# Softmax sums to 128 rows by one on-chip transfer instead of two through memory, with larger booked margins for small transfers

## The chip, the cores and the metric

The kernel runs on one core of a Trainium2 chip. The metric is the device time of one execution in microseconds (us), median of three runs. The engines of the core are named as in the profile: PE is the matrix engine (PEld its weight loads), DVE the vector engine, ACT the scalar engine, POOL the general engine, and SP the engine that issues nearly all transfers here.

## The reference, cut to what matters

A transformer block of 2048 tokens and width 512, in bfloat16: attention with 32 heads of 16 columns, then a gated feed-forward part of inner width 1792. Both are conditioned by a vector `c`.

```python
mod = silu(c) @ w_mod                         # six rows of 512: sa, ca, ga, sb, cb, gb
h = layernorm(x) * (1 + ca) + sa
q, k, v = heads(h @ wqkv)                     # 32 heads of 16
p = softmax(q @ k.T * 16 ** -0.5)
x = x + ga * (merge(p @ v) @ wo)
h = layernorm(x) * (1 + cb) + sb
x = x + gb * ((gelu(h @ w_gate) * (h @ w_up)) @ w_down)
```

## The kernel before, in words

**The main strand.** The queries are cut into six sets (`SETS`: three of 512 tokens, one of 256, two of 128). For each set and each group of four heads (`qd`, a "unit") the score matmuls put slabs of 128 keys by 512 columns into PSUM (`ps_sc`), ACT takes the exponential of two or three slabs by one instruction (`E<-ps_sc`, 128x1024 or 128x1536), and PE multiplies the result with the values (`ps_pv<-E,vaug`). Each head's value columns carry a column of ones, so that the softmax sum comes out as a 17th row. Some rounds are taken from ACT: there DVE makes one slab of the exponential out of the scores by integer arithmetic (`dreg<-ps_sc`, `mreg<-ps_sc`), and four shifted copies of four such slabs (`mreg<-dreg`, `mreg<-mreg`) are multiplied with scaled values (`ps_pv<-mreg,vs`) to even out the error. Four such slabs are a quad. Where a quad has a slab, ACT's instruction has two slabs instead of three.

**The end of a unit** (`unit_end`, L1576). DVE copies the sums of products to `osb`. Rows 16, 48, 80 and 112 of it are the four softmax sums of up to 512 tokens each. So that DVE can invert them on 128 rows instead of four, they are spread: SP writes them to a scratch tensor in memory (`scr_den<-osb`, stream `da`), waits until they are there, and reads them back on 128 rows of `den` (`den<-scr_den`, stream `db`). DVE inverts (`rden<-den`, L352). SP writes the inverse to memory (`scr_rec<-rden`, `dc`) and reads it back four times, once for each head, repeated over 16 rows (`rb<-scr_rec`, `dd`). DVE multiplies (`onorm<-osb,rb`), and for pairs of units SP moves the second's rows beside the first's (`onorm<-onorm`, `de`). The last two units of each of the two last sets take another way (`near_end`, L950): PE spreads the sums with a selection matrix, and DVE inverts them in place.

**The side strands.** When the units of a set are done, the output projection (`side_wo`, L992), the second layer norm and the feed-forward part (`side_ffn`, L1013; `side_down`, L1120) of that set run on PE and DVE beside the scores of the next set, each part with a position in the main strand by which it is due (`plan`, L1187). Weights are streamed from memory by SP. For the last set but one, the side strand does the first eight of the fourteen inner blocks, and `tail_rest` (L1718) the others. After the last scores, `tail` (L1632) finishes the last two sets.

**What sets the order.** All of it is decided while the program is built. `stream` (L1267) keeps an estimate of when each engine is free and when each result is there (`model`, L248) and puts next what can run next. A transfer is booked as there 900 ns after it can start, plus its size by a rate, plus 1000 ns, or 1500 ns where its runs are 64 bytes or less, plus the `MARGIN` (L49) of its stream. An instruction that needs the transfer is put into its engine's order when the estimate says that the data are there; at run time each engine goes through its list in order, and waits where the data are not. So the bookings decide the order of all five lists, and a changed booking moves instructions on all engines. `step` (L1154) picks DVE's and SP's next tasks, and a quad is begun where ACT, DVE and the side strand's credit allow it.

Of the kernel before, what the change touches and what calls it, by code (L numbers as in the profile page):

```python
# [8 lines left out]
FP32 = mybir.dt.float32  # L9
# [4 lines left out]
P = 128  # L14
# [3 lines left out]
DH = 16  # L18
# [27 lines left out]
FLOW = 3  # L46
URGENT = 9
LATE = 2
MARGIN = {"dd": 700, "de": 700}  # L49
EARLY = 2  # L50
BACK = 8
END = (0, None)
# [28 lines left out]
class _Recorder:  # L81
# [21 lines left out]
    def sb(self, name, shape, dt):  # L103
        t = self.nc.alloc_sbuf_tensor(name, shape, dt)
        n = 1
        for s in shape[1:]:
            n *= s
        self.pitch[name] = n * mybir.dt.size(dt)
        self.kind[name] = "sb"
        return t  # L110
# [262 lines left out]
    def dma(self, eng, out, in_, sem, noncontig=False):  # L373
# [8 lines left out]
        run = min(int(a.ap[-1][1]) * mybir.dt.size(a.dtype) for a in (out, in_))  # L382
        return self.rec(eng, fn, [in_], [out], dma=sem, cost=(n, run, MARGIN.get(sem[:2], 0)))

# [36 lines left out]
class _Kernel(_Recorder):  # L421
# [12 lines left out]
    def alloc(self):  # L434
        sb, ps = self.sb, self.ps
        self.xs = sb("xs", [P, NT, D], BF16)
        self.qT = sb("qT", [P, NDC, S_TOK], BF16)
        self.km = [sb("kme", [P, NDC, S_TOK], BF16), sb("kmo", [P, NDC, S_TOK], BF16)]
        self.vaug = sb("vaug", [P, NKT, H * VW], BF16)
        hreg = sb("hreg", [P, NDC * S_TOK], BF16)  # L440
        self.hT = hreg[:, :].rearrange("p (a n) -> p a n", a=NDC)
        self.prodT = hreg[:, 0:NFC * 512].rearrange("p (f n) -> p f n", f=NFC)
        self.prodL = hreg[:, 0:NFC * 256].rearrange("p (f n) -> p f n", f=NFC)
        self.tb2 = hreg[:, 0:4 * D].rearrange("p (t n) -> p t n", t=4)
        self.tb3 = hreg[:, NFC * 512:NFC * 512 + 2 * D].rearrange("p (t n) -> p t n", t=2)
        wreg = sb("wreg", [P, NDC * 1536], BF16)
        self.wqkv = wreg[:, :].rearrange("p (a n) -> p a n", a=NDC)
        self.t2T = wreg[:, 0:NDC * 512].rearrange("p (a n) -> p a n", a=NDC)
        self.gw = wreg[:, 2048:6144].rearrange("p (b k n) -> p b k n", b=2, k=2)
        mreg = sb("mreg", [P, 2 * NDC * F], BF16)  # L450
        self.wst = [[mreg[:, 1024 * (2 * x + b):1024 * (2 * x + b) + 1024].rearrange("p (a n) -> p a n", a=NDC)
                     for b in range(2)] for x in range(2)]
        self.sq = [mreg[:, 4096 + 2048 * i:6144 + 2048 * i] for i in range(NS)]
        self.wmod = mreg[:, 0:NDC * 3072].rearrange("p (a n) -> p a n", a=NDC)
        dreg = sb("dreg", [P, NFC * D], BF16)
        self.tb1 = dreg[:, 0:8 * D].rearrange("p (b t n) -> p b t n", b=2, t=4)
        self.warm = dreg[:, 8 * D:9 * D]
        self.wdst = [dreg[:, a * D:(a + 2) * D] for a in (8, 10, 12)] + [mreg[:, a * D:(a + 2) * D] for a in (2, 0, 6, 4)]
        self.wdst = [a.rearrange("p (f n) -> p f n", f=2) for a in self.wdst]
        self.wg = [self.qT[:, :, 256 * i:256 * i + 256] for i in range(6)]  # L460
        self.wg.append(hreg[:, NFC * 256:NFC * 256 + 1024].rearrange("p (a n) -> p a n", a=NDC))
        self.wu = [self.wst[i // 2][i % 2] for i in range(4)]
        self.wu += [dreg[:, 1024 * i:1024 * i + 1024].rearrange("p (a n) -> p a n", a=NDC) for i in range(4, 7)]
        self.wd = [self.xs[:, 2 * i:2 * i + 2, :] for i in range(6)]
        self.wd.append(hreg[:, NFC * 256 + 1024:NFC * 256 + 2048].rearrange("p (f n) -> p f n", f=2))
        self.kq = [dreg[:, 0:2048], dreg[:, 2048:4096], mreg[:, 12288:14336]]
        self.vs = sb("vs", [P, len(SHIFT), NKT - T0, H * VW], BF16)
        self.wo = sb("wo", [P, 7, D], BF16)
        self.E = sb("E", [P, NSL, 512], BF16)
        self.onorm = sb("onorm", [P, 8, 512], BF16)  # L470
        self.ga = sb("ga", [P, D], BF16)
        self.gb = sb("gb", [P, D], BF16)
        self.xw = self.gw[:, 0, 0, 0:D]
        self.osb = sb("osb", [P, 1024], FP32)
        self.rb = sb("rb", [P, 1024], FP32)
        self.den = sb("den", [P, 4, 16], FP32)
        self.rden = sb("rden", [P, 4, 16], FP32)
        self.mv = sb("mv", [P, NT, 2], FP32)
        self.st6 = sb("st6", [P, 2, 6], FP32)
        self.rstd = sb("rstd", [P, NT], FP32)  # L480
        self.nwx = sb("nwx", [P, NT], FP32)
        self.nwt = sb("nwt", [P, NT], FP32)
        self.crow = dreg[:, 9 * D:10 * D]
        self.tcol = sb("tcol", [P, NDC], FP32)
        self.sc_bf = sb("sc_bf", [P, NDC], BF16)
        self.scbc = dreg[:, 8 * D:9 * D].rearrange("p (a n) -> p a n", a=NDC)
        self.modA = sb("modA", [P, 8], FP32)
        self.modB = sb("modB", [P, 8], FP32)
        self.rm4 = self.den[:, 0, 0:4]
        self.rm = sb("rm", [P, 2], FP32)  # L490
        self.ident = sb("ident", [P, P], BF16)
        self.ones = dreg[:, 10 * D:10 * D + P]
        self.half = dreg[:, 10 * D + P:10 * D + 2 * P]
        self.self32 = sb("self32", [P, P], FP32)
        self.scp = ps("ps_sc", [P, SC, 512], FP32)
        self.pv = ps("ps_pv", [P, 512], FP32)
        self.mi = ps("ps_mi", [P, 512], FP32)
        self.scr1 = self.dram("scr_den", [4, 2048], FP32)
        self.scr2 = self.dram("scr_rec", [4, 2048], FP32)


# [1074 lines left out]
    def unit_end(self, u, acc):  # L1576
        sets, qd, q0, W = u
        b, lo, hi = self.osb_span(u)
        osb, rb = self.osb[:, lo:hi], self.rb[:, lo:hi]
        assert not self.blocked(u)  # L1580
        self.copy("dve", osb, acc[:, 0:W])
        if sets[0] >= len(SETS) - 2 and len(sets) == 1 and qd >= 6:
            self.done(("osb", sets[0], qd))
            return
        self.live[u] = (lo, hi)
        m = 4 * W // P
        o = 8 if BCOL[sets[0]] else 0
        sem = b + 4 * (o > 0)
        pair = (qd - 1, qd) in self.merged(sets[0])
        s1, s2 = self.scr1[b, P * o:P * o + 4 * W], self.scr2[b, P * o:P * o + 4 * W]  # L1590
        den, rden = self.den[:, b, o:o + m], self.rden[:, b, o:o + m]
        steps = [
            ("sp", lambda: self.dma("sp", s1.rearrange("(j n) -> j n", j=4), self.osb[DH:P:32, lo:hi], "da%d" % sem)),
            ("sp", lambda: self.dma("sp", den, s1.rearrange("(p n) -> p n", p=P), "db%d" % sem)),
            lambda: self.recip(rden, den),
            ("sp", lambda: self.dma("sp", s2.rearrange("(p n) -> p n", p=P), rden, "dc%d" % sem)),
            ]
        steps += [("sp", lambda j=j: self.dma(
            "sp", self.rb[32 * j:32 * j + DH, lo:hi],
            s2[W * j:W * j + W].rearrange("(o n) -> o n", o=1).broadcast_to([DH, W]), "dd%d%d" % (sem, j)))  # L1600
            for j in range(4)]

        def fin2():
            c = OCOL[sets[0]]
            self.tt("dve", self.onorm[:, qd, c:c + W], osb, rb, ALU.mult)
            if self.probing is None:
                self.live.pop(u)
                self.done(("half", u))
                if not pair:
                    for k in sets:  # L1610
                        self.done(("onorm", k, qd))

        def merge(j):
            c = OCOL[sets[0]]
            self.dma("sp", self.onorm[32 * j + DH:32 * j + 2 * DH, qd - 1, c:c + W], self.onorm[32 * j:32 * j + DH, qd, c:c + W],
                     "de%d%d" % (qd // 2, j))
            if self.probing is None and j == 3:
                for k in sets:
                    self.done(("onorm", k, qd))

        def free():
            c = OCOL[sets[0]]
            return ("den", u) in self.have and all(
                ("wo", k) in self.have for k in range(sets[0]) if OCOL[k] < c + W and c < OCOL[k] + SETS[k][1])
        self.task(steps, ("den", u))
        self.task([fin2], ("norm", u), free)
        if pair:
            self.task([("sp", lambda j=j: merge(j)) for j in range(4)], None,
                      self.after([("half", u)] + [("onorm", k, qd - 1) for k in sets]))
# [212 lines left out]
```

## Time and profile before

| | |
|---|---|
| three runs | 864.38, 861.86, 860.3 us; median 861.86 |
| the profiled execution | 861.15 us, of which the span on the core is 859.4 us |
| busy, share of the span | ACT 97%, PE 91%, DVE 82%, POOL 1% |
| transfers | 38.97 MB, 45 GB/s over the span |
| waits of DVE for `den` | 6.4 us in 3 places, the longest 3.8 |
| waits of SP for `scr_den<-osb` | 36.5 us in 32 places |

Times in rows are in us unless marked ns. A row of the timeline begins with its start and its length; in brackets behind it stands how long the engine was idle before it, and what ended that. A row of groups ends with the busy time, the mean of one in ns, and the idle time before.

### The profile page before, as it was taken

The page shows a single profiled execution, that of the slowest core. Times are in us where ns is not written, and L with a number is a line of the kernel's source. Part 1 is how long each engine was busy: PE and PEld are TensorE (multiplying, and loading weights), DVE is VectorE, ACT ScalarE, POOL GpSimd, SP SyncE. Part 2 cuts the span into 40 slices and gives each one's busy share as a digit, 9 for nine tenths or more (in the row PEclk, how much of TensorE's full clock was granted, in tenths as well). Part 3 has the DMA queues.
Part 4 walks back from the last instruction along what each step waited for, and adds up shares of the span by engine and source line. Part 5 has one row for each costly group of instructions (what it writes and reads, how often), then busy time and mean ns, then how long its engine had stood idle before and what let it go on. Part 6 is the DMA issues. An engine that isn't in the chain of part 4 may idle for free.

```text
span 859.4 us, 27732 instructions
## 1 busy us (share of the span) xinstructions
PE 781.9 (91%) x12446; PEld 282.9 (33%) x12446; DVE 703.0 (82%) x1363; ACT 829.8 (97%) x747; POOL 4.5 (1%) x12
## 2 busy tenths in 40 slices
PE   7899999988999989999999899999988898998888
PEld 3333332322222222222222222222333333445456
DVE  7855888888998999999998999999985886677354
ACT  6999999999999999999999999999998999999993
POOL 1000000000000000000000000000000000000000
PEclk9999999999999999999998999999998999999999
DMA  9000000000021111210012112110133122041000
GB/s 309 30 15 17 6 10 11 10 13 9 9 64 38 44 38 42 58 34 24 21 32 64 37 33 60 34 57 20 49 94 107 47 69 80 21 123 43 20 7 15
DMA packets 66169, 38.97 MB, mean 45 GB/s; under 512 B 18657, under 2 KB 63906, under 8 KB 66050
## 3 DMA queue, kind: packets, MB, share of 16 engines
q1 hardware_dynamic: 65520, 36.67, 15.2%
q8 instruction: 97, 1.59, 0.8%
q10 hardware_dynamic: 530, 0.53, 0.2%
q14 instruction: 22, 0.18, 0.1%
HBM read 33.81 MB, written 2.61 MB: 42 GB/s over the span
## 4 chain that ended last, share of the span: by engine, by line
ACT 87%; PE 6%; DVE 3%; DMA 2%; SPq 1%; issue 1%; DVEq 0%
ACT E L328 84%; PE ps_sc L315 3%; ACT wreg L328 3%; PE ps_mi L315 2%; SPq L378 1%; PE ps_pv L315 1%; DMA den<-scr_den 1%; DMA xs<-in_A_x_dram 0%; DMA rb<-scr_rec 0%; DVE xs L332 0%; DVE st L368 0%; DMA mreg<-in_B_w_gate_dram 0%; PE ps_mi L319 0%; DVE dreg L340 0%; DVE nwt L332 0%
## 5 line engine op out<-in xcount | busy, mean ns | idle before, releaser
L328 ACT ACTIVATE E<-ps_sc 128x1536 bf16<-128x1536 f32 (+2 forms) x698 | 803.6, 1385 | 16.3 <-PE ps_sc L315 16.2
L315 PE MATMUL ps_sc<-qT,kmo 32*128 32x512 bf16 (+2 forms) x1408 | 173.8, 325 | 20.3 <-ACT E L328 17.3
L315 PE MATMUL ps_sc<-qT,kme 32*128 32x512 bf16 (+2 forms) x1408 | 170.5, 327 | 19.0 <-ACT E L328 16.9
L315 PE MATMUL ps_pv<-E,vaug 128*17 128x512 bf16 (+2 forms) x2416 | 176.0, 319 | 3.1 <-DVE vaug L349 1.4
L340 DVE TENSOR_SCALAR dreg<-ps_sc 128x512 uint16<-128x512 f32 x200 | 137.6, 690 | 31.7 <-PE ps_sc L315 28.4
L340 DVE TENSOR_SCALAR mreg<-dreg 128x2048 uint16<-128x2048 uint16 x200 | 131.8, 681 | 1.0 <-PE ps_pv L315 0.9
L315 PE MATMUL ps_mi<-wreg,mreg 128*32 128x512 bf16 (+2 forms) x1504 | 112.9, 375 | 12.6 <-DVE wreg L345 6.7
L315 PE MATMUL ps_pv<-mreg,vs 128*17 128x512 bf16 (+1 forms) x1344 | 104.5, 355 | 1.0 <-DVE mreg L340 0.8
L315 PEld LDWEIGHTS ps_sc<-qT,kmo 32*128 32x128 bf16 x1408 | 46.8, 92 | 136.2 <-ACT E L328 109.5
L315 PEld LDWEIGHTS ps_sc<-qT,kme 32*128 32x128 bf16 x1408 | 45.8, 92 | 139.1 <-ACT E L328 112.2
L315 PEld LDWEIGHTS ps_pv<-E,vaug 128*17 128x17 bf16 x2416 | 54.9, 89 | 88.3 <-issue 55.4
L340 DVE TENSOR_SCALAR mreg<-ps_sc 128x512 uint16<-128x512 f32 x96 | 66.2, 690 | 15.6 <-PE ps_sc L315 13.6
L340 DVE TENSOR_SCALAR mreg<-mreg 128x2048 uint16<-128x2048 uint16 x96 | 63.2, 683 | 0.0
L315 PEld LDWEIGHTS ps_mi<-wreg,mreg 128*32 128x32 bf16 (+1 forms) x1504 | 34.7, 96 | 59.6 <-issue 21.8
L349 DVE CAST wreg<-ps_mi 128x512 bf16<-128x512 f32 x51 | 35.0, 687 | 12.4 <-PE ps_mi L315 12.0
L345 DVE SCALAR_TENSOR_TENSOR wreg<-wreg,ps_mi 128x512 bf16<-128x512 bf16 x51 | 34.8, 683 | 12.1 <-ACT wreg L328 7.3
L315 PEld LDWEIGHTS ps_pv<-mreg,vs 128*17 128x17 bf16 x1344 | 32.0, 89 | 29.7 <-DVE mreg L340 14.2
L315 PE MATMUL ps_mi<-hreg,wreg 128*32 128x512 bf16 (+1 forms) x496 | 40.4, 377 | 0.7 <-DVE vaug L349 0.6
L332 DVE TENSOR_TENSOR wreg<-wreg 128x1024 bf16<-128x1024 bf16 (+1 forms) x60 | 35.8, 604 | 0.4
L315 PE MATMUL ps_mi<-mreg,hreg 128*32 128x512 bf16 x384 | 32.5, 384 | 0.0
L315 PE MATMUL ps_sc<-xs,ident 128*32 128x512 bf16 x300 | 25.4, 391 | 7.7 <-ACT E L328 7.3
L328 ACT ACTIVATE wreg<-wreg 128x1024 bf16<-128x1024 bf16 (+1 forms) x30 | 31.9, 1068 | 0.0
(149 smaller groups left out, 571.5 us busy)
## 6 DMA issues: line engine op xcount, KB each, us to landing
mreg<-in_B_w_up_dram SPq DMA_DIRECT2D x25, 256.0 KB, 3.2
mreg<-in_B_w_gate_dram SPq DMA_DIRECT2D x21, 256.0 KB, 2.9
rb<-scr_rec SPq DMA_DIRECT2D x96, 32.0 KB, 1.8
mreg<-in_B_w_down_dram SPq DMA_DIRECT2D x12, 256.0 KB, 2.7
dreg<-in_B_w_down_dram SPq DMA_DIRECT2D x9, 256.0 KB, 4.5
mreg<-in_w_mod_dram SPq DMA_DIRECT2D x1, 2048.0 KB, 12.8
out_dram<-xs SPq DMA_DIRECT2D x15, 128.0 KB, 1.7
xs<-in_A_x_dram SPq DMA_DIRECT2D x3, 512.0 KB, 6.5
```

The source lines that it names most:

```text
L315: return self.rec("pe", lambda e: e.matmul(out, lhsT, rhs, start=start, stop=stop, tile_position=tp), [lhsT, rhs], [out], cost=(n, int(rhs ...
L328: return self.rec("act", lambda e: e.activation(out, in_, func, scale=scale, **kw), rd, wr, cost=self.cost("act", out, [in_], "act"))
L332: return self.rec(eng, lambda e: e.tensor_tensor(out, a, b, op), [a, b], [out], cost=self.cost(eng, out, [a, b], "tt"))
L340: return self.rec(eng, lambda e: e.tensor_scalar(out, a, s1, s2, **kw), rd, [out], cost=self.cost(eng, out, [a], "ts") + (60 if len(rd) > ...
L345: return self.rec("dve", lambda e: e.scalar_tensor_tensor(out, a, s, b, op0=op0, op1=op1), rd, [out], cost=self.cost("dve", out, [a, b], " ...
L349: return self.rec(eng, lambda e: e.tensor_copy(out, in_), [in_], [out], cost=self.cost(eng, out, [in_], "ts"))
L378: return e.dma_start(out, in_)
```

## The change

The four rows of sums are now spread over the 128 rows of `den` by one transfer within the chip's memory: each of the four source rows is read as 32 pieces of `m` numbers (64 bytes for a set of 512 tokens, 32 and 16 for the smaller ones), one piece for each row of `den`. The transfer through `scr_den` and the wait between the two are gone. It is stream `db`, whose margin is now 1000 ns (it had none); the margins of `dd` and `de` grow from 700 to 1000 ns.

```diff
-MARGIN = {"dd": 700, "de": 700}
+MARGIN = {"db": 1000, "dd": 1000, "de": 1000}
...
-        self.scr1 = self.dram("scr_den", [4, 2048], FP32)
...
-        s1, s2 = self.scr1[b, P * o:P * o + 4 * W], self.scr2[b, P * o:P * o + 4 * W]
+        s2 = self.scr2[b, P * o:P * o + 4 * W]
...
-            ("sp", lambda: self.dma("sp", s1.rearrange("(j n) -> j n", j=4), self.osb[DH:P:32, lo:hi], "da%d" % sem)),
-            ("sp", lambda: self.dma("sp", den, s1.rearrange("(p n) -> p n", p=P), "db%d" % sem)),
+            ("sp", lambda: self.dma("sp", den, self.osb[DH:P:32, lo:hi].rearrange("j (a n) -> j a n", n=m), "db%d" % sem)),
```

In the built order this moves instructions on every engine from the first set on. The counts that differ: ACT has 356 exponentials of three slabs and 336 of two, where it had 368 and 324; DVE has 308 slabs of its own, where it had 296, and 308 shifted copies, where it had 296; PE has 128 more `ps_pv<-mreg,vs` and 32 more `ps_pv<-dreg,vaug` of 128 columns, both for the last two sets, and fewer filler products (`xs,ident`: 445 for 496); SP has 40 transfers less.

## The prediction

> **What bounds the kernel now.** I read the page first: the busy times, the chain that ended last, and the granted clock.
>
> ```profile
> PE 781.9 (91%) x12446; PEld 282.9 (33%) x12446; DVE 703.0 (82%) x1363; ACT 829.8 (97%) x747; POOL 4.5 (1%) x12
> PEclk9999999999999999999998999999998999999999
> ACT 87%; PE 6%; DVE 3%; DMA 2%; SPq 1%; issue 1%; DVEq 0%
> L340 DVE TENSOR_SCALAR dreg<-ps_sc 128x512 uint16<-128x512 f32 x200 | 137.6, 690 | 31.7 <-PE ps_sc L315 28.4
> L340 DVE TENSOR_SCALAR mreg<-dreg 128x2048 uint16<-128x2048 uint16 x200 | 131.8, 681 | 1.0 <-PE ps_pv L315 0.9
> L349 DVE CAST wreg<-ps_mi 128x512 bf16<-128x512 f32 x51 | 35.0, 687 | 12.4 <-PE ps_mi L315 12.0
> L345 DVE SCALAR_TENSOR_TENSOR wreg<-wreg,ps_mi 128x512 bf16<-128x512 bf16 x51 | 34.8, 683 | 12.1 <-ACT wreg L328 7.3
> ```
>
> ACT is the bound: 97% busy, and 87% of the chain. So a transfer counts only where its lateness reaches ACT (a wait of DVE holds PE, PE holds the next scores), or after the last exponential. Next, ACT's groups with shapes kept apart, and the timeline of ACT, of which these are rows where it waited in the body:
>
> ```profile
> L328 ACT ACTIVATE E<-ps_sc 128x1536 bf16<-128x1536 f32 x368 | 533.1, 1592 | 6.5 <-PE ps_sc L315 6.4
> L328 ACT ACTIVATE E<-ps_sc 128x1024 bf16<-128x1024 f32 x324 | 333.7, 1165 | 2.6 <-PE ps_sc L315 2.6
> L328 ACT ACTIVATE wreg<-wreg 128x512 bf16<-128x512 bf16 x9 | 6.9, 784 | 0.0
> ...
> 460.96 2.54 ACT L328 ACTIVATE E<-ps_sc 128x1024 bf16<-128x1024 f32 x2 [0.49 <-PE ps_sc L315]
> 463.97 1.02 ACT L328 ACTIVATE E<-ps_sc 128x1024 bf16<-128x1024 f32 x1 [0.48 <-PE ps_sc L315]
> 465.49 21.39 ACT L328 ACTIVATE E<-ps_sc 128x1536 bf16<-128x1536 f32 x19 [0.49 <-PE ps_sc L315]
> 657.44 1.45 ACT L328 ACTIVATE E<-ps_sc 128x1536 bf16<-128x1536 f32 x1 [1.54 <-PE ps_sc L315]
> 659.69 1.02 ACT L328 ACTIVATE E<-ps_sc 128x1024 bf16<-128x1024 f32 x1 [0.80 <-PE ps_sc L315]
> 661.21 2.37 ACT L328 ACTIVATE E<-ps_sc 128x1536 bf16<-128x1536 f32 x2 [0.50 <-PE ps_sc L315]
> 664.45 3.71 ACT L328 ACTIVATE E<-ps_sc 128x1536 bf16<-128x1536 f32 x3 [0.87 <-PE ps_sc L315]
> 778.72 1.45 ACT L328 ACTIVATE E<-ps_sc 128x1536 bf16<-128x1536 f32 x1 [0.94 <-PE ps_sc L315]
> 780.33 5.48 ACT L328 ACTIVATE E<-ps_sc 128x1536 bf16<-128x1536 f32 x4 [0.16 <-PE ps_sc L315]
> 805.91 22.94 ACT L328 ACTIVATE E<-ps_sc 128x1536 bf16<-128x1536 f32 x17 [0.61 <-PE ps_sc L315]
> ```
>
> The brackets are all there is to win from waits: 3.71 from 657 to 664, 1.71 from 778 to 806, 1.46 from 460 to 465. The first and the last of these lie in the two slices where PEclk shows 8 (645 to 666, 451 to 473): there PE itself was slower. What made the two later groups, by the timeline of all engines:
>
> ```profile
> 648.65 3.41 SPq L378 DMA_DIRECT2D onorm<-onorm  x4
> 652.10 0.58 SPq L378 DMA_DIRECT2D den<-scr_den  x1
> 652.72 0.43 SPq L378 DMA_DIRECT2D mreg<-in_B_w_gate_dram  x1
> 655.78 1.07 PE L315 MATMUL ps_mi<-wreg,mreg 128*32 128x512 bf16 x16 [1.79 <-DMA mreg<-in_B_w_gate_dram]
> ...
> 776.14 0.20 DVE L352 RECIPROCAL rden<-den 128x8 f32<-128x8 f32 x1 [1.80 <-DMA den<-scr_den]
> ...
> 803.68 0.18 DVE L352 RECIPROCAL rden<-den 128x4 f32<-128x4 f32 x1 [3.82 <-DMA den<-scr_den]
> ```
>
> At 652.72 a weight load stands on SP behind four `onorm` moves and a `den` read, and PE idles 1.79 for it. At 776.14 and 803.68 DVE waits for `den`.
>
> **Part 1, the transfer.** What a unit pays now, in SP's timeline and the transfers' rows:
>
> ```profile
> 103.95 0.53 SPq L378 DMA_DIRECT2D scr_den<-osb  x1
> 105.66 0.34 SPq L378 DMA_DIRECT2D den<-scr_den  x1
> ...
> q1 hardware_dynamic: 65520, 36.67, 15.2%
> den<-scr_den SPq DMA_DIRECT2D x24, 8.0 KB, 1.6
> DVE rden L352 <- DMA den<-scr_den: 6.4, 3, 3.8
> ```
>
> The first transfer costs 1.71 from its issue to the second's. It goes, 40 times, with 40 issues of 0.53 on SP. The trace shows no transfer from four rows of the chip's memory to 128. Its bounds: 1.6 (what the read of the same 128 pieces takes) and 1.6 plus 0.8. The 0.8 is for a transfer that few of the 16 transfer engines share: q1's 65520 packets took 15.2% of 16 times 859.4, so 31.9 ns each, and 24 more packets in a row take 0.77. I take 2.4. The code books 0.90 + 0.04 + 1.50 + 1.00 = 3.44 for it, where it booked 1.93 and 2.44 for the two; so the planner counts on the sums 0.93 earlier, and the real ones come about 1 before they are counted on. `dd` and `de` get 0.3 more each, so `onorm` is counted on 0.3 to 0.6 earlier. By itself all this is worth nothing to ACT; of the saving only DVE's waits for `den` reach it, 1.71. They go; if that cover is gone, they are back.
>
> There is one rule that speaks against the change. The Trainium skill ("DMA: Bandwidth & Descriptors", "Why a DMA increments its semaphore by 16 and not by 1") says that a transfer is shared by as many engines as divide the outermost sizes of both its sides, so here by 4 and not 16. By it the transfer takes the upper bound above; by 16 engines it would take the lower. No row here shows which. Both lie under the booking, so the sum is the same, but the chance of the slower rival below is larger for it.
>
> **Part 2, the order.** The new lists are in the built kernel. Three differences bear on ACT.
>
> - Three more quads, all in the last three sets: 12 exponentials go from three slabs to two, 12 x (1592 - 1165) = **-5.1**. The price on DVE is 12 x 690 and 12 x 681, 16 in all. DVE has 156 free over the span; in the last stretch this isn't free, see below.
> - In the third weight transition the gate load now stands ahead of the four moves and just behind the `den` transfer, so PE's 1.79 goes, and I count the slow stretch behind it with it, since the clock is down only where PE had stood: -3.7 (1.54, the first bracket alone, if the clock goes down anyway). With the 1.7 from `den` this is **-5.4**.
> - New waits in other places are to be expected, since all lists are new. Nearest rows: one group like that at 460 to 465 (1.46) and one wait like that at 778.72 (0.94): **+2.4**. From nothing to twice the 6.9 lost now.
>
> Until the end of the third set ACT has the same work in both kernels.
>
> **Part 3, the end.** Here the change costs. The rows of the end:
>
> ```profile
> 830.93 8.35 ACT L328 ACTIVATE E<-ps_sc 128x1536 bf16<-128x1536 f32 x6
> 832.38 0.17 DVE L352 RECIPROCAL rden<-den 128x4 f32<-128x4 f32 x1
> 834.82 0.96 DVE L352 RECIPROCAL rb<-ps_mi 128x128 f32<-128x128 f32 x1 [0.58 <-PE ps_mi L315]
> 838.72 0.29 DVE L332 TENSOR_TENSOR onorm<-osb,rb 128x128 bf16<-128x128 f32 x1 [2.62 <-DMA rb<-scr_rec]
> 839.77 0.29 DVE L349 COPY osb<-ps_pv 128x128 f32<-128x128 f32 x1 [0.76 <-PE ps_pv L315]
> 842.76 0.69 DVE L368 BATCH_NORM_STATS2 st<-ps_sc 128x6 f32<-128x512 f32 x1
> 843.70 0.15 DVE L340 TENSOR_SCALAR nwx<-mv 128x1 f32<-128x1 f32 x1
> 827.99 0.43 DVE L332 TENSOR_TENSOR wreg<-wreg 128x512 bf16<-128x512 bf16 x1
> 828.45 0.29 DVE L340 TENSOR_SCALAR wreg<-wreg 128x512 bf16<-128x512 bf16 x1
> ```
>
> The last exponential ends at 839.28, the last `osb` at 840.06, the first step of the last norm starts at 843.70, 3.64 behind `osb`. In the new lists the output projection of the last set but one begins at 98.7% of the scores, where it began at 97.5%. So its feed-forward part slides past the last scores:
>
> - two of ACT's nine 0.784 functions now stand behind the last exponential: -1.6 before it;
> - between the last `osb` and the first norm step DVE has in addition a cast (0.69, of which 0.55 lies in the wait for PE), three products of 0.43, a scaling of 0.29, two `onorm` of 0.29, an inverse of 0.96, two combinations of 0.68 and one more product: 5.1;
> - the waits in this order (PE's two projections of 16 products, ACT's function) and for the last `rb`: from its inverse at 832.38 to its `onorm` at 838.72 it is 6.3 now, and in the new list the place of that `onorm` is some 6 behind the inverse: about 1.3;
> - behind the last DVE slab, about 13.9 before the last exponential's end, DVE has some 13.5 of work, so the last `osb` comes some 0.9 later behind ACT's end than now.
>
> That is 5.1 + 1.3 + 0.9 = **+7.3** behind the scores, and **-1.6** ahead of them.
>
> **The sum.** -5.1 - 5.4 + 2.4 - 1.6 + 7.3 = -2.4, against the profiled execution's own 861.15: 858.7. That lies within the three runs of before, whose median is 861.86.
>
> **The rivals.**
>
> - *The end hides its work, and no new waits come.* The 5.1 stay, the 1.3, 0.9 and 2.4 don't: -5.1 - 5.4 - 1.6 + 5.1 = -7.0, 854.1. For it: longer margins, and DVE's wait of 2.62 for `rb` in the end now. Against it: the new list has that same wait in another place.
> - *The new transfer lands later than it is booked, slower than before.* It decides from 3.4 on, twice the 1.6 of the read. Then DVE stands at each of 40 inverses, and behind it all its slabs, casts and copies, for which PE waits. Now 1.8 + 3.8 of such waits (6.4 in all) cost ACT 1.71, 0.27 for each us; 1 too late 40 times costs 10.7: 869.4. For it: 776.14, where the read was late behind weight loads. Against it: 2.4 is the upper bound from the rows.
> - *The wait is hidden anyway.* SP isn't the bound, the removed 1.71 lies in its waits, and the waits of ACT only change places: 5.4 lost again in place of 2.4, 861.7; up to 867 with twice as much.
>
> **How the numbers follow.** Forecast 0.38 (854.5 to 863), the good end 0.27 (851 to 857), the late transfer 0.15 (865 and more), the changed places 0.20 (860 to 867). Half a per cent, about what a measurement of this kernel tells from no change, is 857.55 to 866.2. Faster: 0.27 and a third of the forecast, 0.40. Slower: 0.15 and a quarter of the last, 0.20. The rest is 0.40. The range is 851 to 868: it leaves out most of the late transfer and the best of the good end.
>
> **What would show it.** ACT busy near 824.7 and its last three-slab exponential ending near 830; no wait of PE for the gate load in the third transition; waits of DVE for `den` under 2 in all; landing of `den<-osb` 1.6 to 2.4; from the last exponential to the end of the span some 27 for 20 now. It is wrong if `den<-osb` lands later than 3.4, if ACT waits more than 7 in the body, or if the end takes under 24 or over 30.

## The result and the profile after

The changed kernel takes 856.99 us (median of nine runs, 854.64 to 859.58) against 861.86 for the kernel before, timed beside it. The ratio is 0.9941, interval 0.992 to 0.9961: some 0.6% faster, 4.9 us. The profiled execution has a span of 855.9 where before has 859.4, so it shows 3.5 of this.

The page of the changed kernel: busy times, granted clock, chain.

```profile
PE 778.6 (91%) x12532; PEld 282.9 (33%) x12534; DVE 716.4 (84%) x1387; ACT 824.1 (96%) x747; POOL 4.5 (1%) x12
PEclk9999999999999999999999999999999999999999
ACT 85%; PE 8%; DVE 4%; DMA 2%; issue 0%; SPq 0%; DVEq 0%
```

ACT is still the bound. It is busy 5.7 less and DVE 13.4 more. The two slices of lower clock are gone from the row, but a slice is 21 us long and shows a 9 at 0.92 too, the clock of 645 to 666 here, so it hides short stretches. The table by stretches, taken in steps of 1 us, shows that PE's clock was at 0.50 (half clock) for 6.8 us from 458.7 and again from 656.7 in before, and for 3.4 us from 657.9 and again from 808.1 in this kernel. Rows from within these stretches, one of before and two of after (length, busy time of PE, PEld, DVE, ACT, POOL, then clock, DMA share, GB/s):

```profile
459.00:465.00 6.00, 6.00 (x47) 2.35 (x44) 4.09 (x9) 4.96 (x5) 0.00 (x0) 0.50 0.01 2
```

```profile
658.00:661.00 3.00, 3.00 (x40) 0.66 (x36) 1.58 (x4) 1.43 (x2) 0.00 (x0) 0.50 0.01 1
809.00:811.00 2.00, 2.00 (x48) 1.10 (x44) 1.41 (x2) 1.23 (x2) 0.00 (x0) 0.50 0.00 0
```

ACT's groups with shapes kept apart (busy, then mean ns of one, then idle before):

```profile
L328 ACT ACTIVATE E<-ps_sc 128x1536 bf16<-128x1536 f32 x356 | 523.0, 1597 | 4.4 <-PE ps_sc L315 4.3
L328 ACT ACTIVATE E<-ps_sc 128x1024 bf16<-128x1024 f32 x336 | 351.2, 1175 | 2.2 <-PE ps_sc L315 2.2
```

Twelve exponentials went from three slabs to two, as the lists said. The timeline of ACT, the rows after 75 us with a wait of it in the body:

```profile
267.04 21.36 ACT L328 ACTIVATE E<-ps_sc 128x1536 bf16<-128x1536 f32 x19 [0.18 <-PE ps_sc L315]
370.34 2.37 ACT L328 ACTIVATE E<-ps_sc 128x1024 bf16<-128x1024 f32 x2 [0.35 <-PE ps_sc L315]
659.57 4.19 ACT L328 ACTIVATE E<-ps_sc 128x1536 bf16<-128x1536 f32 x3 [2.86 <-PE ps_sc L315]
678.95 10.49 ACT L328 ACTIVATE E<-ps_sc 128x1024 bf16<-128x1024 f32 x9 [0.23 <-PE ps_sc L315]
781.92 0.63 ACT L328 ACTIVATE wreg<-wreg 128x512 bf16<-128x512 bf16 x1 [1.40 <-DVE wreg L332]
810.36 20.87 ACT L328 ACTIVATE E<-ps_sc 128x1024 bf16<-128x1024 f32 x18 [0.77 <-PE ps_sc L315]
```

These are 5.8, where the brackets of before from 460 on were 6.9. What DVE waited for among the transfers of the sums (total, times, longest):

```profile
DVE onorm L332 <- DMA rb<-scr_rec: 13.5, 4, 4.4
```

Of the waits for `den`, 6.4 in before, 0.2 is left, but the waits for `rb`, the other transfer of the same chain, grew from 5.9 to 13.5. DVE's own rows show what two of them did:

```profile
777.72 0.42 DVE L332 TENSOR_TENSOR onorm<-osb,rb 128x256 bf16<-128x256 f32 x1 [2.16 <-DMA rb<-scr_rec]
781.52 0.71 DVE L332 TENSOR_TENSOR wreg<-wreg 128x512 bf16<-128x512 bf16 x2
804.35 0.29 DVE L332 TENSOR_TENSOR onorm<-osb,rb 128x128 bf16<-128x128 f32 x1 [4.38 <-DMA rb<-scr_rec]
```

From 777.72 on DVE works without a gap to 781.52, whose product ACT's function of 781.92 waits for: 2.16 of late transfer came out as 1.40 on ACT. Behind the 4.38 ACT lost 0.77, at 810.36 and so within the half-clock stretch from 808.1; how much of it is the late transfer's isn't told apart.

The largest wait of ACT stands in the third weight transition. The timeline of all engines there:

```profile
645.14 0.48 SPq L378 DMA_DIRECT2D mreg<-in_B_w_gate_dram  x1
646.45 3.78 SPq L378 DMA_DIRECT2D onorm<-onorm  x4
...
652.40 0.47 SPq L378 DMA_DIRECT2D mreg<-in_B_w_gate_dram  x1
652.92 1.89 SPq L378 DMA_DIRECT2D rb<-scr_rec  x4
654.85 1.14 SPq L378 DMA_DIRECT2D mreg<-in_B_w_gate_dram  x1
657.46 1.52 PE L315 MATMUL ps_mi<-wreg,mreg 128*32 128x512 bf16 x16 [2.48 <-DMA mreg<-in_B_w_gate_dram]
```

The first gate load is indeed ahead of the four moves now. PE waits for another one instead. The third, issued at 654.85 behind four `rb` reads, looks like the one, but the view of the gate loads, limited to the one issued at 652.40, names the second:

```profile
  PE ps_mi L315: 2.5, 1
DMA to landing us min/median/max: 4.9/4.9/4.9
```

It is ahead of the `rb` reads and lands 4.9 after its issue, at 657.3, when PE goes on; the third lands at 658.6 and nobody waits for it. Just ahead of the second, from 650.90 on, SP had issued three loads `dreg<-in_B_w_down_dram` of 256 KB. In all 13 traces of this document the second gate load stands right behind these three. It took 4.2 to 5.5 to land in twelve of them; in the other (the margin of 1100 below) the issues of the three were spread over 2.73 instead of some 1.5, it took 3.4, and PE didn't wait for it. The one that PE waited for in before, at 652.72, took 2.9. That the three loads delay the second is likely by this, but no run moved them.

The end, again all engines:

```profile
817.60 13.63 ACT L328 ACTIVATE E<-ps_sc 128x1536 bf16<-128x1536 f32 x10
831.95 0.29 DVE L349 COPY osb<-ps_pv 128x128 f32<-128x128 f32 x1 [1.58 <-PE ps_pv L315]
832.65 0.61 ACT L328 ACTIVATE wreg<-wreg 128x512 bf16<-128x512 bf16 x1
835.27 0.63 ACT L328 ACTIVATE wreg<-wreg 128x512 bf16<-128x512 bf16 x1 [0.31 <-DVE wreg L332]
836.57 0.28 DVE L332 TENSOR_TENSOR onorm<-osb,rb 128x128 bf16<-128x128 f32 x1
840.21 0.15 DVE L340 TENSOR_SCALAR nwx<-mv 128x1 f32<-128x1 f32 x1
```

The last exponential ends at 831.23 (839.28 before), 8.05 earlier. The first step of the last norm, at 840.21, begins 7.97 behind the last `osb`, where it was 3.64. From the last exponential to the end of the span it is 24.7, for 20.1. So -8.05 and +4.55 (rounded) give the -3.5.

### The profile page after: what moved, and what is told of

Its sections match the earlier page's. It is cut to its first block, busy times and chain, and to the rows that moved or that the text cites. A ratio compares the mean times of both kernels' runs of the same rounds, so it can differ in the third digit from the quotient of the medians.

```text
span 855.9 us, 27893 instructions
## 1 busy us (share of the span) xinstructions
PE 778.6 (91%) x12532; PEld 282.9 (33%) x12534; DVE 716.4 (84%) x1387; ACT 824.1 (96%) x747; POOL 4.5 (1%) x12
## 4 chain that ended last, share of the span: by engine, by line
ACT 85%; PE 8%; DVE 4%; DMA 2%; issue 0%; SPq 0%; DVEq 0%
ACT E L328 82%; PE ps_sc L315 3%; PE ps_mi L315 3%; ACT wreg L328 2%; PE ps_pv L315 1%; DVE wreg L345 1%; DMA scr_rec<-rden 1%; DMA mreg<-in_B_w_gate_dram 1%; DVE mreg L340 0%; DVE wreg L349 0%; SPq L378 0%; DMA xs<-in_A_x_dram 0%; DVE st L368 0%; DVE wreg L332 0%; PE ps_mi L319 0%
## 5 line engine op out<-in xcount | busy, mean ns | idle before, releaser
L328 ACT ACTIVATE E<-ps_sc 128x1536 bf16<-128x1536 f32 (+2 forms) x698 | 797.3, 1385 | 13.6 <-PE ps_sc L315 13.4
L315 PE MATMUL ps_sc<-qT,kmo 32*128 32x512 bf16 (+2 forms) x1408 | 176.8, 323 | 17.9 <-ACT E L328 15.5
L315 PE MATMUL ps_pv<-E,vaug 128*17 128x512 bf16 (+2 forms) x2376 | 171.6, 320 | 3.9 <-DVE vaug L349 1.4
L340 DVE TENSOR_SCALAR dreg<-ps_sc 128x512 uint16<-128x512 f32 x208 | 143.1, 689 | 28.4 <-PE ps_sc L315 24.8
L340 DVE TENSOR_SCALAR mreg<-dreg 128x2048 uint16<-128x2048 uint16 x208 | 136.2, 680 | 0.1
L315 PE MATMUL ps_pv<-mreg,vs 128*17 128x512 bf16 (+2 forms) x1504 | 107.9, 341 | 1.2 <-DVE mreg L340 1.0
L340 DVE TENSOR_SCALAR mreg<-ps_sc 128x512 uint16<-128x512 f32 x100 | 68.9, 690 | 15.2 <-PE ps_sc L315 13.2
L340 DVE TENSOR_SCALAR mreg<-mreg 128x2048 uint16<-128x2048 uint16 x100 | 66.2, 683 | 0.0
L315 PEld LDWEIGHTS ps_pv<-mreg,vs 128*17 128x17 bf16 x1504 | 34.5, 89 | 31.8 <-DVE mreg L340 13.4
L332 DVE TENSOR_TENSOR onorm<-osb,rb 128x512 bf16<-128x512 f32 (+2 forms) x44 | 23.7, 538 | 13.6 <-DMA rb<-scr_rec 13.5
```

Of the source, the lines that this page charges most:

```text
L315: return self.rec("pe", lambda e: e.matmul(out, lhsT, rhs, start=start, stop=stop, tile_position=tp), [lhsT, rhs], [out], cost=(n, int(rhs ...
L328: return self.rec("act", lambda e: e.activation(out, in_, func, scale=scale, **kw), rd, wr, cost=self.cost("act", out, [in_], "act"))
L332: return self.rec(eng, lambda e: e.tensor_tensor(out, a, b, op), [a, b], [out], cost=self.cost(eng, out, [a, b], "tt"))
L340: return self.rec(eng, lambda e: e.tensor_scalar(out, a, s1, s2, **kw), rd, [out], cost=self.cost(eng, out, [a], "ts") + (60 if len(rd) > ...
```

## The experiments

The prediction's theory was that the new order does the work (twelve shorter exponentials, a better place of the gate load, against a longer end) and that the transfer itself is worth only the 1.7 of ACT's waits behind late `den`. The rival came from the result: the transfer itself is worth about 4, in any order. The first two kernels take the two apart, since the lists of instructions can be kept while only the transfer is exchanged. Where ACT's waits are summed below, these are the brackets of its timeline from 13 us up to its last three- or two-slab exponential: 9.0 in before, 7.9 in after.

**The old order with one transfer.** Before's lists of every engine; the transfer to memory isn't issued and not waited for.

```diff
-                    e.wait_ge(self.sem[s], v)
+                    if s[:4] != "d_da":
+                        e.wait_ge(self.sem[s], v)
+                if op.stream[:4] == "d_da":
+                    return
...
-  self.dma("sp", den, s1.rearrange("(p n) -> p n", p=P), "db%d" % sem)
+  e.dma_start(den, self.osb[DH:P:32, lo:hi].rearrange("j (a n) -> j a n", n=m))
```

> Every engine's list is that of the kernel before; only what SP does differs: the transfer to scr_den isn't issued, SP doesn't wait for it, and den is filled from osb on chip. Theory A (the new order makes the gain, the transfer itself is worth at most the 1.7 of ACT's waits at 778 to 806): 860 to 862, ratio 0.998 to 1.000. Rival B (the shorter path itself makes it): 857, ratio 0.994. In both, DVE's waits for den fall from 6.4 to under 3.

Measured: 857.55 us, ratio 0.9956 (0.9937 to 0.9975). Its last exponential ends at 835.70, 3.6 earlier than before's, and its end is before's 20.1. Its waits of DVE for the two transfers:

```profile
DVE onorm L332 <- DMA rb<-scr_rec: 8.5, 4, 3.2
DVE rden L352 <- DMA den<-osb: 3.4, 2, 2.9
```

And two waits of ACT in its timeline, of a sum of 5.9:

```profile
655.25 1.45 ACT L328 ACTIVATE E<-ps_sc 128x1536 bf16<-128x1536 f32 x1 [1.13 <-PE ps_sc L315]
813.08 12.20 ACT L328 ACTIVATE E<-ps_sc 128x1536 bf16<-128x1536 f32 x9 [0.80 <-PE ps_sc L315]
```

The transfer alone, in an order that isn't made for it, is worth 4.3 of the 4.9. ACT's waits fall by 3.2, in three places: the three waits at 460 to 466 are gone (1.46), the third transition costs 2.61 for 3.71, and the stretch from 776 on 1.09 for 1.71. Only the last is what the forecast credited to the transfer, and DVE's waits for `den` halved without going. Of the first place the row of 459 to 465 tells more, beside the one of before shown above:

```profile
459.00:465.00 6.00, 5.67 (x74) 2.18 (x71) 5.55 (x12) 6.00 (x7) 0.00 (x0) 1.00 0.20 56
```

With the transfer changed and the lists kept, the clock stays up there and ACT has no idle time. The clock is at 0.50 in two other places, for 3.4 us each, from 655.8 and from 809.4. How a transfer bears on the clock isn't shown by these rows.

**The new order with two transfers.** After's lists; the one step on SP writes `scr_den`, waits for it and reads it back.

```diff
+        def two(e):
+            n = self.hop[sem] = self.hop.get(sem, 0) + 16
+            e.dma_start(s1.rearrange("(j n) -> j n", j=4), self.osb[DH:P:32, lo:hi]).then_inc(self.sem["hop%d" % sem], 16)
+            e.wait_ge(self.sem["hop%d" % sem], n)
+            return e.dma_start(den, s1.rearrange("(p n) -> p n", p=P))
```

> Every engine's list is that of the changed kernel; only what SP does differs: where the one transfer stood, SP writes to scr_den, waits, and reads den back. Theory A: 857 to 859, since the two transfers (1.7 + 1.6) just fill the 3.44 that are booked. Rival B: 861 to 862, the whole gain gone. DVE's waits for den above the 0.2 of the changed kernel, some 3 to 10.

Measured: 864.85 us, ratio 1.0042 (1.0021 to 1.0063), slower than before. ACT's waits sum to 13.2, and the last exponential ends at 838.38. SP's wait for the first transfer, in total:

```profile
SPq L1601 <- DMA scr_den<-osb: 49.5, 40, 3.2
```

The timeline of all engines shows early in the run how that reaches ACT:

```profile
74.78 0.53 SPq L1599 DMA_DIRECT2D scr_den<-osb  x1
76.50 0.33 SPq L1601 DMA_DIRECT2D den<-scr_den  x1
76.95 1.75 SPq L378 DMA_DIRECT2D rb<-scr_rec  x4
...
81.66 0.69 DVE L332 TENSOR_TENSOR onorm<-osb,rb 128x512 bf16<-128x512 f32 x1 [1.81 <-DMA rb<-scr_rec]
...
83.42 0.40 PE L315 MATMUL ps_mi<-mreg,dreg 128*32 128x512 bf16 x4 [1.58 <-DVE dreg L340]
...
84.18 1.45 ACT L328 ACTIVATE E<-ps_sc 128x1536 bf16<-128x1536 f32 x1 [1.47 <-PE ps_sc L315]
```

SP stands between its two issues, and behind it stand the four `rb` reads of another unit. They go out 1.57 later than in after, and three of the four take 3.3 to 3.8 to land, where in after all took 1.8 to 2.0; why they are slower isn't shown. DVE waits at `onorm`, PE for DVE's next product, and ACT 1.47 for the scores behind that. In after the four reads go out right behind the one issue:

```profile
75.38 1.78 SPq L378 DMA_DIRECT2D rb<-scr_rec  x4
```

There `onorm` has no wait, and ACT none. So in this order the one transfer is worth 7.9 against two issued in one step (5.3 of it in ACT's waits). This is an upper bound for what the transfer is worth, since the kernel is harsher than a mere undoing: before's own list put other issues between the two, at this place the `rb` reads, and SP stood for the first transfer 36.5 in 32 places, here 49.5 in 40. What the new order alone is worth is read from the pair with one transfer, 857.55 to 856.99: nothing that can be told.

**One transfer, with the old margins.** After, with `MARGIN = {"dd": 700, "de": 700}`: the transfer changes, the margins don't.

> The one transfer with the margins of before (700 for dd and de, none for db). The built lists have 12 exponentials fewer of three slabs and two of ACT's functions behind the last scores, as the changed kernel has. Theory A: 855 to 859 from these counts. Rival C (the margins make the gain by fewer late transfers): 861 to 864, with more waits of DVE for den and rb than the 13.7 of the changed kernel.

Measured: 856.16 us, ratio 0.9942 (0.9924 to 0.996). It is another order once more: DVE waits 3.8 for `rb` and 1.0 for `den`, ACT's waits sum to 5.6, the last exponential ends at 829.34, the end takes 24.2. The larger margins add nothing to the transfer.

**Two transfers, with the new margins.** Before, with `MARGIN = {"db": 1000, "dd": 1000, "de": 1000}`.

> Two transfers through scr_den as before, with the margins of the changed kernel. The built lists have 12 exponentials fewer of three slabs too, and none of ACT's functions behind the last scores, so the shorter end of the kernel before. Theory A: 853 to 858 (before, less 5.1 of ACT's work, plus or minus its waits). Rival B: 862 or more, as the path is the old one. Rival C: 857.

Measured: 853.26 us, ratio 0.9915 (0.9888 to 0.9941). By the medians the margins without the transfer give 3.7 more than the change does; the two intervals overlap (0.992 to 0.9961 for the change). The order has the same 356 and 336 exponentials as after, no function of ACT behind the last scores, and an end of 20.1; the last exponential ends at 831.47. Its one wait of DVE for a transfer of the sums:

```profile
DVE onorm L332 <- DMA rb<-scr_rec: 0.7, 1, 0.7
```

**One transfer in that order.** The first experiment's edit, on the kernel just shown.

> Every engine's list is that of e4 (two transfers booked, new margins); SP issues only the one transfer on chip, as in e1. In e4 DVE waited for neither den nor rb. Theory A (the transfer is worth the waits of DVE that it takes away, and what these drag into PE and ACT): nothing to win here, 852 to 855, within 1 of e4's 853.3. Rival B (it is worth some 4 whatever the order, as from before to e1: fewer transfers, SP free sooner): 849 to 850.

Measured: 852.38 us, ratio 0.9902 (0.9881 to 0.9924), the fastest of all kernels here. ACT's waits for scores, first with two transfers, then with one:

```profile
ACT E L328 <- PE ps_sc L315: 13.2, 14, 2.1
```

```profile
ACT E L328 <- PE ps_sc L315: 12.6, 13, 2.1
```

The transfer is worth 0.9 here, less than the two intervals can tell from nothing, where it was worth 4.3 and 7.9. With that the rival falls: the transfer has no price of its own. It pays where an order has late transfers or a queue that stands for them, and this one has hardly any late ones.

**Booked too early.** After, with `"db": -1500`, so that the planner counts on `den` 2.5 earlier than in after.

> The changed kernel with the booking of den<-osb cut from 3.44 to 0.94 (margin -1500), so that DVE's inverses stand before the data can be there and the end of each wait shows when the transfer lands. If it is shared by 16 engines: 1.6 from issue to the inverse; if by 4: 2.4; in no case under 1. Most of the 40 inverses then wait, 0.7 to 1.5 each, 25 to 60 in all. By the price of 0.27 of ACT for each us of DVE's wait that is 7 to 16 more: 864 to 873. If ACT is covered better than that, 857 to 862.

Measured: 858.64 us, ratio 0.9976 (0.9955 to 0.9997). The bulk of the expectation was missed; its covered branch (857 to 862) came. DVE waited 21 times, and two of these cases are shown, one early and one late:

```profile
DVE rden L352 <- DMA den<-osb: 21.0, 21, 3.0
```

```profile
67.74 0.68 SPq L378 DMA_DIRECT2D den<-osb  x1
69.67 0.25 DVE L352 RECIPROCAL rden<-den 128x16 f32<-128x16 f32 x1 [1.03 <-DMA den<-osb]
...
789.59 0.18 DVE L352 RECIPROCAL rden<-den 128x4 f32<-128x4 f32 x1 [2.98 <-DMA den<-osb]
791.85 1.45 ACT L328 ACTIVATE E<-ps_sc 128x1536 bf16<-128x1536 f32 x1 [0.85 <-PE ps_sc L315]
```

This gives what no other trace does, the time of the new transfer: from SP's issue to the inverse that waited for it 1.93 here, 1.81 to 1.93 in 17 of the 21 cases, the median 1.87, the longest 2.95. It also bears on the price of a late one. The waits before 600 us cost ACT nothing here. The three late ones (2.42 at 767, 2.98 at 789, 2.34 at 798) were followed by waits of ACT of 1.59, 0.85 and 1.54. Against after, the kernel with 21 us of waits is 1.7 slower by the medians and 3 by the ratios, with eight three-slab exponentials more and another end in the same sum, so this is no clean price.

**A margin for the transfer behind it.** After's late waits are those for `rb`, which is read back from `scr_rec`. After, with `"dc": 1000` for that write.

> The changed kernel with 1000 more booked for scr_rec<-rden too. The built lists have 8 exponentials fewer of three slabs than before (12 in the changed kernel) and no function of ACT behind the last scores. DVE's waits for rb fall from 13.5 to under 5. If late transfers and the sliding end are what is left to win: 851 to 854, like e4. If only the exponentials taken from ACT count: 858 to 860.

Measured: 857.45 us, ratio 0.9954 (0.9936 to 0.9972). Missed: 851 to 854 was expected. DVE has no wait for `rb` or `den` left at all, but the order has 360 and 332 exponentials, and ACT waits elsewhere:

```profile
662.41 1.45 ACT L328 ACTIVATE E<-ps_sc 128x1536 bf16<-128x1536 f32 x1 [2.44 <-PE ps_sc L315]
```

Ahead of this PE had stood 2.4 for a gate load, as in after. No late transfers of the sums is thus not enough to be fast.

**A tenth of a microsecond.** After, with `"db": 1100`: how far does an order swing when nothing of substance changes?

> The changed kernel with 1100 in place of 1000 for the margin of den<-osb alone, a tenth of a us. The transfer is the same; the lists come out new (the same counts of exponentials, two of ACT's functions behind the last scores). If a booking acts by how late data are: 856 to 858, as the changed kernel. If any change of a booking draws a new order with its own waits: off by 2 to 5 in either direction.

Measured: 856.29 us, ratio 0.9951 (0.9933 to 0.9969). The total stays, its parts don't: the last exponential ends at 827.33, 3.9 earlier than in after, and the end takes 27.2, 2.5 more. DVE waits 2.9 for `rb` instead of 13.5, PE doesn't wait for a gate load, and the clock stays up to the last exponential.

**The gate load ahead of the `rb` reads.** After, with the third gate load of the third transition moved ahead of the four `rb` in SP's list; nothing else moves.

```diff
+    def ahead(self):
+        sp = [op for op in self.ops if op.eng == "sp"]
+        gate = [op for op in sp if op.stream in ("d_st00", "d_st01")]
+        for op in gate[16:16 + 1]:
+            j = sp.index(op)
+            while sp[j - 1].stream[:4] in ("d_dd", "d_da"):
+                j -= 1
...
```

> The changed kernel, all lists as they are, but in SP's list one weight load moved: in the third transition the third gate load stands ahead of the four rb transfers in place of behind them. In the changed kernel it was issued at 654.85, and PE waited 2.48 and then ACT 2.86 for it. If the wait is the place on SP, the load goes out at about 652.9, PE waits under 0.7, ACT under 1.2, and the time is 855.0 to 855.9. If the load is late for another reason (its buffer, the transfer engines), nothing moves: 856.5 to 857.5.

Measured: 855.22 us, ratio 0.9938 (0.9919 to 0.9957): nothing that can be told from after. The same place in the timeline of all engines:

```profile
653.64 1.95 SPq L378 DMA_DIRECT2D mreg<-in_B_w_gate_dram  x2
655.64 2.98 SPq L378 DMA_DIRECT2D rb<-scr_rec  x4
658.61 1.90 PE L315 MATMUL ps_mi<-wreg,mreg 128*32 128x512 bf16 x16 [2.56 <-DMA mreg<-in_B_w_gate_dram]
661.09 2.79 ACT L328 ACTIVATE E<-ps_sc 128x1536 bf16<-128x1536 f32 x2 [3.31 <-PE ps_sc L315]
```

PE waits as long as ever, and two readings of the trace say why. The load that PE waits for is again the second, issued at 653.64 right behind the three `dreg` loads and landed 4.8 later, at 658.4; the move didn't touch it. And the load that was moved goes out no earlier: SP stands 1.1 for PE's product of 654.13 (`ps_mi`, which reads a buffer of `mreg`) and issues it at 655.2, where after issued it at 654.85. So the queue of `rb` reads was not the cause, and this experiment doesn't test what was: the place of the second gate load behind the three `dreg` loads. Moving these wasn't tried.

**The same move in the fastest kernel.**

> The same move on e5 (order of e4, one transfer), where PE waited 1.49 and ACT 1.00 for that load. By the place on SP: 851.0 to 851.9, the fastest of all. Otherwise 852.4, as e5.

Measured: 852.7 us, ratio 0.9904 (0.9873 to 0.9935). PE's wait for the load goes from 1.49 to 1.2, ACT's from 1.00 to 0.74; in the time nothing shows. Here too PE waits for the second load, which the move doesn't touch (5.3 and then 5.0 from issue to landing).

**Before once more,** one run, to see which of its waits and slow slices are its own.

> The kernel before, unchanged, for a second profile. In the first, ACT waited 9.0 in the body, 1.46 of it at 460 to 465 and part of the 3.71 at 657 to 664 with the granted clock at 8 tenths. If these belong to the order, both come back: 859 to 863 with 8 to 10 of waits. If the clock's dips are of that execution alone, the waits are 5.5 to 7.5 and the clock row is all nines.

Measured: 862.02 us. Its clock by slices:

```profile
PEclk9999999999999999999998999999999999999899
```

The dip in the 22nd slice and the three waits of ACT at 460 to 466 come again, the clock at 0.50 for 6.8 us as before. The one at 656.7 doesn't, and two of 3.4 us, from 803.5 and from 813.8, are new. At 645 to 666 the clock is 1.00, by the table of stretches, PE still waits 1.65 for the gate load, and ACT 1.33 in two brackets, the first:

```profile
657.07 1.45 ACT L328 ACTIVATE E<-ps_sc 128x1536 bf16<-128x1536 f32 x1 [1.16 <-PE ps_sc L315]
```

So the half-clock stretches differ between executions of one kernel, and the time differs with them. Every run's mean granted clock is on record. In the 72 runs of before beside the experiments the median time goes from 857.3 at 1.000 (4 runs) over 858.59 at 0.998 (5), 859.76 at 0.996 (13) and 862.17 at 0.992 (16) to 865.7 at 0.986 (3). One stretch of 3.4 us takes 0.002 off the mean clock, and goes with some 1.2 us here. At the same mean clock, with few runs each:

| mean clock | before | after | old order, one transfer |
|---|---|---|---|
| 0.998 | 858.59 | 856.11 | 856.21 |
| 0.996 | 859.76 | 857.33 | 857.55 |

So at the same clock the change is worth some 2.5 and the transfer in the old order some 2.3; the other half of the 4.9 goes with fewer half-clock stretches (the median run of before is at 0.993, of after at 0.998). Whether the transfer makes these fewer, or both follow from PE's waits, isn't shown.

## Why the prediction was right, and where it wasn't

The forecast was -2.4 by its own execution, 858.7, and the same executions show -3.5. The total was near, and this was luck in part: up to the last exponential it gained 8.05 where 9.7 was forecast (-5.1, -3.0 and -1.6), the end lost 4.55 where 7.3 was, and the two misses cancel but for 1.1.

- **The step that failed:** "By itself all this is worth nothing to ACT; of the saving only DVE's waits for `den` reach it, 1.71." With the order kept, the transfer was worth 4.3 in the old lists, of which the `den` waits can't have given more than 0.62 in ACT's brackets; in the new lists it was worth up to 7.9, and 0.9 where hardly anything was late. The forecast followed the transfer only to the inverse that waits for it. The runs showed a second way, in the new lists: what stands on SP behind the transfer's issue is late as well (the `rb` reads at 76.95), and comes out at ACT. In the old lists it is the clock: of the 3.2 that ACT's waits fell there, 1.46 and 1.10 lie where a half-clock stretch of 6.8 went (458.7) and another one shrank to 3.4 (656.7), which no step foresaw. Whether the transfer brought this, and how, stays open.
- **The order.** It was priced as the source of the gain: -5.1, -1.6 and the gate load's -3.7, against +7.3. With one transfer in both, it is worth nothing that can be told.
- **The exponentials, -5.1:** right. ACT is busy 5.7 less, and twelve have changed their form.
- **The waits, -5.4 and +2.4, so -3.0:** -1.1 was measured (9.0 to 7.9). Term by term: the gate load, -3.7 forecast, gave 3.71 to 2.86, since PE now waits for another load of the same stream, the second, which lands 4.9 after its issue; the `den` waits did go, but waits for `rb` behind 777 and 804 put 1.40 and 0.77 in place of the 1.71; the three waits at 460 to 466, which the forecast let stand, went (-1.46), and 0.76 of small new ones came.
- **The clock.** The forecast made the lower clock at 645 to 666 a consequence of PE's standing there. In the repeat of before PE stands there too, 1.65 for 1.79, at a clock of 1.00, and ACT loses 1.33 in place of 3.71. So PE's standing isn't enough to bring it. It isn't needed either: ahead of 458.7 PE had no wait above 0.53 within 10 us. Whether it takes part stays open, since in after half clock begins 0.4 behind the end of PE's 2.48. So 2.4 of the 3.7 was no sure gain, and the 1.54 kept for that case would have been the better price. The stretch at 458.7 recurs in the repeat and is in none of the other traces.
- **The end, +7.3:** the mechanism was right and the size too large. +4.55 was measured. The work that slid is there, row by row, and the two functions stand behind the last exponential (1.24 for 1.6). But the last `onorm` at 836.57 waits for no `rb` (1.3 had been counted), a part of the work lies in waits that were there anyway (+4.3 for 6.4 of both), and the last `osb` came 0.2 later behind ACT's end, not 0.9.
- **The transfer itself:** 1.87, between the bounds of 1.6 and 2.4 and below the 3.44 booked. The rule of the Trainium skill that was weighed ("DMA: Bandwidth & Descriptors", "Why a DMA increments its semaphore by 16 and not by 1") can't be decided by it: the trace lists no landing for a transfer with a side of four rows, and 1.87 contains DVE's start as well.
- **The rivals.** A late transfer didn't come. Its price, 0.27 of ACT for each microsecond of DVE, was too high: the early booking's 21 of waits went with 1.7 to 3 more, 0.08 to 0.14 for each, other differences of that order included. What one costs depends on its place: in that kernel the early ones were free, in the new order with two transfers one of 1.81 at 81 us cost 1.47. "The waits change places" came true in part, for `den` and `rb`. The good end, 854.1, is what the margins alone reached, in an order of their own.

Of the prediction's own signs, ACT's busy time (824.1) and the end (24.7) came out in its bounds, and "no wait of PE for the gate load" didn't (2.48).

What holds over the runs: where transfers are late, the shorter one pays. What doesn't: that an order's gain can be read from the parts that differ. After, 1.1 in place of 1.0, the old margins and the margin for `scr_rec` lie within 1.3 us of each other (856.16 to 857.45), with last exponentials ending from 827.3 to 834.4 and, for the first three, ends from 24.2 to 27.2. That the order of the new margins with two transfers is 3 to 4 better goes with `rb` hardly late and a short end, but what leads the planner there isn't shown, and 853.26 is one draw among them. The version to keep is that order with the one transfer: 852.38, ratio 0.9902 (0.9881 to 0.9924), though it can't be told from the 853.26 with two.

## What to carry to other kernels

To price one edit under a planner, build it twice in fixed lists, the old order with the new transfer and the new order with the old one: here this turned "the order gains, the transfer does nothing" around for the order of the changed kernel, where the transfer made the gain. Follow a transfer along the queue that issues it as well as to the engine that waits for it: what stands behind it there (here the `rb` reads) can be what the bound engine feels. And a latency that a planner books is a lever of the same size as the transfer itself, in both directions and hard to foresee, so try margins alone before crediting the operation. Before a transfer is blamed for a wait, find out which issue it was, by limiting the view to one issue and reading its landing: the issue nearest to the wait was the wrong one here, and two experiments moved it for nothing. And compare runs at the same granted clock, or say how much of a difference goes with it.

## What was unexpected of the hardware

The four-row to 128-row transfer within the chip took 1.87 (median of 21) from issue to use, where the write to memory and the issue of the read behind it alone had taken 1.71; its one issue holds SP 0.59, where the two held it 0.53 and 0.34.

PE's clock fell to 0.50 for 3.4 or 6.8 us at a time. It did so once or more ahead of the last exponential in 12 of the 13 traces here, in a program that keeps PE 91% busy. A stretch of 6.8 came at the same place in both executions of before (from 458.7), and one in the first alone (from 656.7), although PE's wait ahead of that was much the same in both, 1.79 and 1.65. A group of 16 products that takes 1.05 at full clock took 1.52 where it ran partly in such a stretch (657.46 in after).

A gate load of 256 KB that SP issues right behind three loads of that size took 4.2 to 5.5 to land in twelve traces; the others of the same transition took 2.7 to 4.6.
